# Cosformer attention and a gated MLP on one core: batch 0 in two halves of four heads, chunk 0's first product in units of 128 tokens by four column blocks

## The chip, the cores and the metric

One Trainium2 chip, one core of it. The metric is the device time of one execution in microseconds; less is better. The kernel is written out engine by engine: TensorE (matmuls and their weight loads), VectorE (DVE), ScalarE (ACT), GpSimd (POOL, which here mainly issues loads) and SyncE (SP, which issues stores and transposing DMAs).

## What is computed

Two stages, with 8 batches, 8 heads, 576 positions, head width 64, so 4608 tokens of 512 values; the inner width of the second stage is 2048.

```
def phi(x, c, s):                      # c, s: cos and sin of pi/2 * pos / 576
    r = np.maximum(x, 0.0)
    return np.concatenate([r * c, r * s], axis=-1)
q_p, k_p = phi(q, ...), phi(k, ...)
kv  = einsum('bhsf,bhsd->bhfd', k_p, v);  z = k_p.sum(axis=2)
x   = einsum('bhsf,bhfd->bhsd', q_p, kv) / (einsum('bhsf,bhf->bhs', q_p, z) + 1e-6)
h   = x @ w_in                         # x as [4608, 512], w_in [512, 2048]
out = (h * cos(h)) @ w_out             # w_out [2048, 512]
```

## The kernel before

**Loads.** POOL issues all of them, in the order written, and the values become f16 on the way. K and V of a batch lie as 116 rows of five positions for each head, q as 96 rows of six. Batch 0's loads are split, then come the four column groups of w_in (512 tokens' first product needs all four), two groups of w_out, batch 1, the other two of w_out. Eight semaphores are used in turn, so that a load is issued once the eighth before it has landed.

**Attention of one batch.**
- `scaled` (L143 on DVE, L138 on ScalarE): relu times cos or sin, for one position group `i` of q or k; two instructions each, `t` = 0 and 1.
- `spread_v` (L196, L198): copies V into `vz`, whose 65th column is one, so that the same matmul gives the sum z. For batch 0 there is no such copy: `kv_head` reads a strided view of V and of a block of ones behind it, 128 columns wide (L219).
- `kv_head` (L209, L219): five matmuls for each head into `KV`; after four heads ScalarE copies the result to `kvz` (L224).
- `q_turn` (L167): eight TensorE transposes for one `i` into `QT`, copied to `X` (batch 0 on ScalarE, L186, one `i` at a time; batch 1 two at a time, L181 on ScalarE and L176 on DVE).
- `num_tile` (L235): for 128 tokens, eight matmuls of 65 columns into `NP`; then on DVE `dn` (L242), the reciprocal `rd` (L246) and the product `x` (L255), which `normalise` may issue in two parts.
- `x_turn` (L273): four transposes of `x` into `XP`, copied into `XT` (L281 on ScalarE, L279 on DVE).

From batch 2 on the transposes are DMAs that SP issues.

**The MLP** runs in nine chunks of 512 tokens. M1 (`m1_group`, L288): for each of 16 column blocks of 128 four matmuls of w_in against `XT`; then `co` = cos(M1) on ScalarE (L294) and `g` = M1 · `co` on DVE (L297). M2 (`m2_part`, L307): for each of four token groups `m` sixteen matmuls in four parts, copied by ScalarE to `ost` (L314) and stored by SP. Chunk 0's M1 goes over the 16 blocks twice, 256 tokens at a time, so that it may begin when two token tiles are there.

**Order.** It is written by hand. Chunk c has steps s; `at(c, s, f)` places a piece of attention behind step s, and each engine takes its own instructions in that order. The attention of batches 0 and 1 stands within chunk 0, whose M1 has 32 steps and whose M2 has 16; `z` is the first step of M2. Chunk 1 needs tokens 512 to 1023, that is the last tile of batch 0 and four tiles of batch 1. `warm` issues matmuls on zeros, to keep TensorE running while loads come in.

**PSUM.** `psM` has tags m1 and m2 with two banks each; M1 takes them in turn, M2 of `m` = 0 and 1 takes m2. `psA` has one tag, `att`, with two buffers of two banks, for `QT`, `KV`, `NP` and `XP`.

Of the kernel before, what the change touches and what calls it, by code (L numbers as in the profile page):

```python
# [17 lines left out]
def kernel(  # L18
# [55 lines left out]
    VB = [cpool.tile([PK, H * RUNK + D], F16, name=f"v{n}") for n in "ab"]  # L74
# [23 lines left out]
    def load_q(b, i0=0, i1=R):  # L98
        dst = st[b]["q16"].rearrange("p (h r) -> p h r", h=H)
        nc.gpsimd.dma_start(  # L100
            out=dst[:, :, i0 * D:i1 * D],
            in_=q[b].rearrange("h (p i) d -> p h (i d)", i=R)[:, :, i0 * D:i1 * D],
        )
# [23 lines left out]
    def scaled(b, which, i, h0=0, h1=H):  # L127
        s = st[b]
        rows, n, o = (PR, R, 0) if which == "q" else (PK, RK, R)
        if which + "p" not in s:  # L130
            s[which + "p"] = apool.tile([rows, n, H * F], F16, name=which + "p",
                                        tag=which + "p", bufs=1)
        dst = s[which + "p"][:, i].rearrange("p (h t d) -> p h t d", t=2, d=D)
        src = s[which + "16"][:, 0:H * n * D].rearrange("p (h i d) -> p h i d", i=n, d=D)
        cs = CS[0:rows, :, o + i:o + i + 1]
        for t in range(2):
            if b == 0 and (which == "k" and h0 == 4 and t == 1 or which == "q" and i == 4):
                nc.scalar.activation(  # L138
                    out=dst[:, h0:h1, t, :], in_=src[:, h0:h1, i, :], func=AF.Relu,
                    scale=cs[:, t],  # L140
                )
                continue
            nc.vector.tensor_scalar(  # L143
                out=dst[:, h0:h1, t, :], in0=src[:, h0:h1, i, :],
                scalar1=0.0, scalar2=cs[:, t],
                op0=ALU.max, op1=ALU.mult,
            )

    def q_turn(b, i, tag="m1"):
        s = st[b]  # L150
        if i == 0:
            s["X"] = apool.tile([P, H, S], F16, name="X", tag="X")
        if b >= 2:
            nc.sync.dma_start_transpose(
                out=s["X"][:, :, i * PR:(i + 1) * PR], in_=s["qp"][:, i],
            )
            return
        if b == 1:
            if i % 2 == 0:
                s["QT"] = psA.tile([P, 2, H, P], F16, name="QT", tag="att")  # L160
            QT = s["QT"][:, i % 2]
        elif i >= 4:
            QT = psA.tile([P, 2, H, P], F16, name="QT", tag="att")[:, 0]
        else:
            QT = psM.tile([P, H, P], F16, name="QT", tag=tag)
        for h in range(H):
            nc.tensor.matmul(  # L167
                QT[:, h, 0:PR], lhsT=s["qp"][:, i, h * F:(h + 1) * F], rhs=ID[0:PR, 0:PR],
                is_transpose=True,
            )  # L170
        if b == 1 and i % 2 == 0:
            return
        i0 = i - (b == 1)
        dst = s["X"][:, :, i0 * PR:(i + 1) * PR]
        if b == 1 and i > 1:
            nc.vector.tensor_copy(  # L176
                out=dst.rearrange("p h (a c) -> p a h c", a=2),
                in_=s["QT"][:, :, :, 0:PR],
            )
        elif b == 1:  # L180
            nc.scalar.activation(  # L181
                out=dst.rearrange("p h (a c) -> p a h c", a=2),
                in_=s["QT"][:, :, :, 0:PR], func=AF.Copy,
            )
        else:
            nc.scalar.activation(out=dst, in_=QT[:, :, 0:PR], func=AF.Copy)  # L186

    def spread_v(b, h):
        s = st[b]
        if h == 0:  # L190
            s["vz"] = apool.tile([PK, H, RK, VS], F16, name="vz", tag="vz", bufs=1)
            nc.gpsimd.memset(s["vz"][:, :, :, D:VS], 1.0)
        src = s["v16"][:, 0:H * RUNK].rearrange("p (h i d) -> p h i d", i=RK, d=D)
        dst = s["vz"][:, h:h + 2, :, 0:D]
        if b != 2:
            nc.scalar.activation(out=dst, in_=src[:, h:h + 2], func=AF.Copy)  # L196
        else:
            nc.vector.tensor_copy(out=dst, in_=src[:, h:h + 2])  # L198

    def kv_head(b, h):  # L200
# [5 lines left out]
        n = P if b == 0 else D + 1  # L206
        for i in range(RK):
            if b > 0:
                nc.tensor.matmul(  # L209
                    s["KV"][:, h, 0:n], lhsT=s["kp"][:, i, h * F:(h + 1) * F],  # L210
                    rhs=s["vz"][:, h, i, 0:n], start=(i == 0), stop=(i == RK - 1),
                )
                continue
            base = s["v16"][:, h * RUNK + i * D: h * RUNK + (i + 1) * D]
            vz = bass.AP(
                tensor=base.tensor, offset=base.offset,
                ap=[list(base.ap[0]), [H * RUNK - h * RUNK - i * D, 2], [1, D]],
            )
            nc.tensor.matmul(  # L219
                s["KV"][:, h], lhsT=s["kp"][:, i, h * F:(h + 1) * F], rhs=vz,  # L220
                start=(i == 0), stop=(i == RK - 1),
            )
        if h % 4 == 3:
            nc.scalar.activation(  # L224
                out=s["kvz"][:, h - 3:h + 1], in_=s["KV"][:, h - 3:h + 1, 0:D + 1],
                func=AF.Copy,
            )

# [31 lines left out]
    def x_turn(b, t):  # L260
# [6 lines left out]
        if b == 0 and t < 2:  # L267
            XPf = psM.tile([P, 1024], F16, name="XP", tag="m1")
        else:
            XPf = psA.tile([P, 2048], F16, name="XP", tag="att")  # L270
# [7 lines left out]
        if b == 0 and t == 1:  # L278
# [4 lines left out]
    def m1_group(c, j, n0=0, n1=CH):  # L283
        if ("g", c) not in st:
            st["g", c] = gpool.tile([P, NJT, CH], F16, name="g", tag="g")
        M1 = psM.tile([P, CH], F32, name="M1", tag=("m1", "m2")[j % 2])
        for i in range(NCT):
            nc.tensor.matmul(  # L288
                M1[:, n0:n1], lhsT=w_in_sb[:, i, j * P:(j + 1) * P],
                rhs=XT[:, i, c * CH + n0:c * CH + n1],  # L290
# [4 lines left out]
            out=co[:, n0:n1], in_=M1[:, n0:n1], func=AF.Sin, bias=PIH, scale=1.0,  # L295
        )
        nc.vector.tensor_tensor(  # L297
            out=st["g", c][:, j, n0:n1], in0=M1[:, n0:n1], in1=co[:, n0:n1], op=ALU.mult,
# [31 lines left out]
    HS = NJT  # L330
# [11 lines left out]
    def plan_stage0():  # L342
        at(0, 1, q_turn, 0, 4)
        at(0, 2, scaled, 0, "q", 5)
        at(0, 3, x_turn, 0, 2)
        at(0, 4, loads, 2, "kvq")
        at(0, 6, q_turn, 0, 5)
        for t, n in ((3, 9), (4, HS + 6)):
            at(0, n, num_tile, 0, t, False)
            at(0, n + 1, normalise, 0, t, 0, 1)  # L350
            at(0, n + 2, normalise, 0, t, 1, 2)
            at(0, n + 5, x_turn, 0, t)
        z = 2 * HS
        for i in range(R):
            if i < RK:
                at(0, z + i // 2, scaled, 1, "k", i)
            at(0, z + 3 + i // 2, scaled, 1, "q", i)
        for n in range(4):
            at(0, z + 1 + n, spread_v, 1, 2 * n)
        for h in range(4):  # L360
            at(0, z + 4, kv_head, 1, h)
        for i in range(2):
            at(0, z + 5, q_turn, 1, i)
        for h in range(4, H):
            at(0, z + 5, kv_head, 1, h)
        for i in range(2, R):
            at(0, z + 5 + i // 2, q_turn, 1, i)
        for n, f, t in ((7, num_tile, 0), (8, num_tile, 1), (9, x_turn, 0),
                        (10, num_tile, 2), (10, x_turn, 1), (12, num_tile, 3),
                        (13, x_turn, 2), (14, x_turn, 3), (14, num_tile, 4)):  # L370
            at(0, z + n, f, 1, t)
        at(1, 2, x_turn, 1, 4)
        for i, n in enumerate((9, 10, 11, 12, 13)):
            at(0, z + n, scaled, 2, "k", i)
        for n in range(4):
            at(0, z + 12 + n, spread_v, 2, 2 * n)
# [40 lines left out]
    with tc.manual_schedule():  # L417
# [11 lines left out]
        load_kv(0, "k", 0, 4)  # L429
        load_rest(0, "k")  # L430
        load_kv(0, "k", 4, 8)
        load_q(0, 0, 4)
        for h in range(0, H, 2):
            if h == 2:
                load_rest(0, "v")
            load_kv(0, "v", h, h + 2)
        nc.gpsimd.memset(st[0]["v16"][:, H * RUNK:], 1.0)
        load_w_in(0)
        load_q(0, 4, R)
# [13 lines left out]
        warm(33)  # L453
        for h0 in (0, 4):
            for i in range(RK):
                scaled(0, "k", i, h0, h0 + 4)
        for i in range(4):
            scaled(0, "q", i)
            if i < 2:
                q_turn(0, i)  # L460
        for h in range(8):
            kv_head(0, h)
        q_turn(0, 2, "m2")
        num_tile(0, 0)
        q_turn(0, 3)
        warm(1)
        num_tile(0, 1)
        warm(3)
        x_turn(0, 0)
        warm(2)  # L470
        scaled(0, "q", 4)
        x_turn(0, 1)
        num_tile(0, 2)
        for s in range(2 * HS):
            n = s // HS * (CH // 2)
            m1_group(0, s % HS, n, n + CH // 2)
# [3 lines left out]
        for s, (m, g) in enumerate(order):  # L480
            m2_part(0, m, g)
            run(0, 2 * HS + s)
# [38 lines left out]
```

## Time and profile before

| | us |
|---|---|
| median of 3 runs | 301.39 (300.96 to 301.56) |
| the profiled execution, its own time | 299.56 |
| its span, first to last instruction | 297.8 |
| first matmul of chunk 0's M1 | 19.19 |
| first matmul of chunk 0's M2 | 36.71 |
| first matmul of chunk 1's M1 | 56.52 |

The profile counts time from the first instruction. A line of the timeline is start, length, engine, source line, operation, out<-in, shape, count, and in brackets the idle time before it with what ended it. A group row is a line, engine and operation with its shape and count, then busy time and the mean ns of one, then the idle time before. A DMA row is the number of issues, the KB of one (in f16, as they arrive) and the median time from issue to landing.

### The profile page before, as it was taken

What the parts mean: (1) busy time and instruction counts of PE and PEld (TensorE: products, weight loads), DVE (VectorE), ACT (ScalarE), POOL (GpSimd) and SP (SyncE); (2) the same over time, 40 slices, a digit from 0 to 9 for tenths busy, and PEclk for the clock granted to TensorE, in tenths of its full rate; (3) what the DMA queues carried; (4) which work ended last, traced back from release to release, by engine and by line L of the source; (5) the groups of instructions that cost most, each with busy time, mean ns of one, the idle gap of its engine ahead of it and who ended that gap; (6) DMA issues with size and microseconds to landing.
All of it is one profiled execution on the core that took longest, in us unless ns stands there. A gap on an engine that the chain in (4) does not pass through costs nothing.

```text
span 297.8 us, 5456 instructions
## 1 busy us (share of the span) xinstructions
PE 290.4 (98%) x2031; PEld 150.9 (51%) x2031; DVE 190.3 (64%) x470; ACT 158.7 (53%) x261; POOL 39.8 (13%) x65
## 2 busy tenths in 40 slices
PE   8999999999999999999999999999999999999994
PEld 3577756554544544455445544554455444444441
DVE  1668987988489666966686768677766267007600
ACT  1589952676357624762477158715771177137511
POOL 8733310005004002100210022000000000000000
PEclk9999999999999999999999999999999999999999
DMA  6999999589999996996799959996702610121022
GB/s 89 181 203 206 200 206 200 155 108 134 188 170 147 179 186 117 199 168 130 123 165 181 149 116 169 161 163 136 163 16 70 118 35 0 41 76 28 0 73 70
DMA packets 78019, 38.84 MB, mean 130 GB/s; under 512 B 48296, under 2 KB 73384, under 8 KB 77992
## 3 DMA queue, kind: packets, MB, share of 16 engines
q0 software_dynamic: 28240, 18.36, 44.1%
q1 hardware_dynamic: 49752, 20.13, 38.6%
q8 instruction: 16, 0.26, 0.4%
q14 instruction: 11, 0.09, 0.1%
HBM read 36.76 MB, written 9.44 MB: 155 GB/s over the span
## 4 chain that ended last, share of the span: by engine, by line
PE 89%; DVE 5%; DMA 3%; ACT 1%; POOL 1%; issue 1%; ACTq 0%; POOLq 0%
PE M L307 42%; PE M L288 38%; PE NP L235 3%; DVE g L297 3%; PE KV L209 3%; DMA q<-in_q_dram 3%; PE QT L167 1%; ACT co L294 1%; PE KV L219 1%; PE XP L273 1%; DVE qp L143 1%; POOL ka L108 1%; DVE x L255 0%; PE W L451 0%; POOL ka L115 0%
## 5 line engine op out<-in xcount | busy, mean ns | idle before, releaser
L297 DVE TENSOR_TENSOR g<-M,co 128x512 f16<-128x512 f32 (+1 forms) x160 | 99.9, 635 | 57.5 <-ACT co L294 57.4
L307 PE MATMUL M<-w_out_sb,g 128*128 128x512 f16 x576 | 132.3, 379 | 0.1
L288 PE MATMUL M<-XT,w_in_sb 128*128 128x512 f16 (+1 forms) x640 | 129.5, 358 | 0.6 <-DVE dn L242 0.3
L294 ACT ACTIVATE co<-M,PIH 128x512 f32<-128x512 f32 (+1 forms) x160 | 101.9, 647 | 27.5 <-PE M L288 27.0
L288 PEld LDWEIGHTS <-w_in_sb 128*128 128x128 f16 x640 | 61.3, 98 | 59.7 <-issue 0.9
L307 PEld LDWEIGHTS <-g 128*128 128x128 f16 x576 | 53.8, 98 | 58.7 <-issue 0.3
L314 ACT ACTIVATE ost<-M 128x512 f32<-128x512 f32 x36 | 21.5, 597 | 93.4 <-PE M L307 68.4
L255 DVE TENSOR_TENSOR x<-NP,rd 128x512 f16<-128x512 f32 (+1 forms) x42 | 27.9, 664 | 4.9 <-DMA XT<-x 3.6
L143 DVE TENSOR_SCALAR qp<-q,CS 96x512 f16<-96x512 f16 x94 | 28.5, 350 | 2.1 <-DMA q<-in_q_dram 1.2
L143 DVE TENSOR_SCALAR kp<-ka,CS 116x512 f16<-116x512 f16 (+1 forms) x75 | 21.6, 345 | 5.4 <-DMA ka<-in_k_dram 5.4
L235 PEld LDWEIGHTS <-X 128*128 128x128 f16 x320 | 15.3, 98 | 8.7 <-issue 0.8
L100 POOL DMA_DIRECT2D q<-in_q_dram x9 | 7.0, 779 | 90.8 <-DVE qp L143 88.2
L235 PE MATMUL NP<-kvz,X 128*128 128x65 f16 x320 | 17.0, 194 | 0.2 <-issue 0.2
L242 DVE TENSOR_SCALAR dn<-NP 128x8 f32<-128x8 f32 x40 | 6.5, 162 | 15.4 <-PE NP L235 15.2
L196 ACT ACTIVATE vz<-va 116x640 f16<-116x640 f16 x20 | 13.5, 727 | 0.0
L451 PE MATMUL W<-WU 128*128 128x512 f16 x39 | 12.0, 470 | 1.2 <-DVE PIH L426 1.2
L209 PEld LDWEIGHTS <-kp 116*128 116x128 f16 x280 | 10.7, 98 | 3.1
L209 PE MATMUL KV<-vz,kp 116*128 116x65 f16 x280 | 11.2, 193 | 0.0
L246 DVE RECIPROCAL rd<-dn 128x8 f32<-128x8 f32 x40 | 8.1, 203 | 1.4
L108 POOL DMA_DIRECT2D ka<-in_k_dram x8 | 6.5, 817 | 18.3 <-DVE kp L143 14.9
L451 PEld LDWEIGHTS <-WU 128*128 128x128 f16 x39 | 4.4, 117 | 7.2 <-issue 3.9
L224 ACT ACTIVATE kvz<-KV 128x260 f16<-128x260 f32 x16 | 6.2, 387 | 3.3 <-PE KV L209 2.3
(35 smaller groups left out, 74.5 us busy)
## 6 DMA issues: line engine op xcount, KB each, us to landing
out_dram<-ost SPq DMA_DIRECT2D x24, 192.0 KB, 2.3
q<-in_q_dram POOLq DMA_DIRECT2D x7, 576.0 KB, 7.6
ka<-in_k_dram POOLq DMA_DIRECT2D x6, 560.0 KB, 13.2
va<-in_v_dram POOLq DMA_DIRECT2D x6, 560.0 KB, 11.8
out_dram<-ost SPq DMA_DIRECT2D x24, 128.0 KB, 5.9
w_in_sb<-in_moe_w_in_dram POOLq DMA_DIRECT2D x4, 512.0 KB, 9.9
w_out_sb<-in_moe_w_out_dram POOLq DMA_DIRECT2D x4, 512.0 KB, 16.7
out_dram<-ost SPq DMA_DIRECT2D x24, 64.0 KB, 3.1
```

Source lines behind the costliest of these rows:

```text
L108: nc.gpsimd.dma_start(out=rows_of(st[b][which + "16"])[0:FULL, h0:h1], in_=full[:, h0:h1],)
L143: nc.vector.tensor_scalar(out=dst[:, h0:h1, t, :], in0=src[:, h0:h1, i, :], scalar1=0.0, scalar2=cs[:, t], op0=ALU.max, op1=ALU.mult,)
L196: nc.scalar.activation(out=dst, in_=src[:, h:h + 2], func=AF.Copy)
L209: nc.tensor.matmul(s["KV"][:, h, 0:n], lhsT=s["kp"][:, i, h * F:(h + 1) * F], rhs=s["vz"][:, h, i, 0:n], start=(i == 0), stop=(i == RK - 1),)
L235: nc.tensor.matmul(NP[:, h // 4, o:o + D + 1], lhsT=s["X"][:, h, c0:c0 + P], rhs=s["kvz"][:, h], start=True, stop=True,)
L255: nc.vector.tensor_tensor(out=x4[:, a0:a1], in0=np4[:, a0:a1, :, 0:D], in1=rd[:, a0:a1].broadcast_to((P, a1 - a0, 4, D)), op=ALU.mult,)
L288: nc.tensor.matmul(M1[:, n0:n1], lhsT=w_in_sb[:, i, j * P:(j + 1) * P], rhs=XT[:, i, c * CH + n0:c * CH + n1], start=(i == 0), stop=(i == ...
L294: nc.scalar.activation(out=co[:, n0:n1], in_=M1[:, n0:n1], func=AF.Sin, bias=PIH, scale=1.0,)
L297: nc.vector.tensor_tensor(out=st["g", c][:, j, n0:n1], in0=M1[:, n0:n1], in1=co[:, n0:n1], op=ALU.mult,)
L307: nc.tensor.matmul(M2, lhsT=st["g", c][:, j, m * P:(m + 1) * P], rhs=w_out_sb[:, j], start=(j == 0), stop=(j == NJT - 1),)
L314: nc.scalar.activation(out=ost, in_=M2, func=AF.Copy)
L451: nc.tensor.matmul(W, lhsT=WU[:, 0:P], rhs=WU, start=True, stop=True)
```

## The change

- Batch 0 is loaded in halves of four heads, in the order K, q, V of the first half, then K, q, V of the second (the V of the second in two pieces), then w_in. q comes with all six positions of four heads, where before it came with four positions of all heads and the other two later.
- Batch 0's scalings, transposes (`q_half`, two positions of four heads to a bank), KV products and the first token tile (`first_half`, `first_turn`) are done for each half. Batch 0's V is spread on DVE like that of the other batches, and the ones are set by DVE.
- Chunk 0's M1 runs in 16 units (`m1_unit`): 128 tokens by four column blocks, sixteen matmuls of 128 columns into one bank, one `co` and one `g` of 512 columns. The order of the units is `units`; unit 0 needs token tile 0 alone.
- Token tile 1's and 2's `x_turn` move into M1 (within units 0 and 1), and `num_tile` 2 behind unit 0; `num_tile` 3 stands behind unit 6 and its `x_turn` behind unit 8; tile 4 behind units 9 to 13.
- For batch 1, every odd position of q has its second scaling on ScalarE, and two of the four spread copies go from ScalarE to DVE. Its KV products stand behind steps z+5 and z+6, its transposes behind z+7 to z+9, `num_tile` 0 to 4 behind z+8, 9, 10, 12 and 15 (before: z+4 and z+5; z+5 to z+7; z+7, 8, 10, 12 and 14).
- The opening's matmuls on zeros are 25, then 2, 1, 3, 4 and 2 (before: 33, then 1, 3 and 2).

```diff
-            if b == 0 and (which == "k" and h0 == 4 and t == 1 or which == "q" and i == 4):
+            if t == 1 and (b == 0 and which == "k" and i < (4 if h0 else 3)
+                           or b == 1 and which == "q" and i % 2):
                 nc.scalar.activation(   # scaled, on ScalarE
...
-        if b != 2:
+        if b > 2 or b == 1 and h < 4:
             nc.scalar.activation(out=dst, in_=src[:, h:h + 2], func=AF.Copy)   # spread_v
...
+    def q_half(h0, i, pool, tag):
+        QT = pool.tile([P, 2, 4, P], F16, name="QT", tag=tag)
+        for a in range(2):
+            turn(0, QT[:, a], i + a, h0)
...
+    def m1_unit(u, k_, t):
+        M1 = psM.tile([P, 4, P], F32, name="M1", tag=("m1", "m2")[u % 2])
+        for j in range(4):
+            for i in range(NCT):
+                f0 = (4 * k_ + j) * P
+                nc.tensor.matmul(
+                    M1[:, j], lhsT=w_in_sb[:, i, f0:f0 + P],
+                    rhs=XT[:, i, t * P:(t + 1) * P],
+                    start=(i == 0), stop=(i == NCT - 1),
+                )
+        if u == 0:
+            x_turn(0, 1)
+            num_tile(0, 2)
+        if u == 1:
+            x_turn(0, 2)
+        co = opool.tile([P, 4, P], F32, name="co", tag="co")
+        nc.scalar.activation(out=co, in_=M1, func=AF.Sin, bias=PIH, scale=1.0)
+        nc.vector.tensor_tensor(
+            out=g_for(0)[:, 4 * k_:4 * k_ + 4, t * P:(t + 1) * P], in0=M1, in1=co,
+            op=ALU.mult,
+        )
...
-        load_kv(0, "k", 0, 4)
-        load_rest(0, "k")
-        load_kv(0, "k", 4, 8)
-        load_q(0, 0, 4)
-        for h in range(0, H, 2):
-            if h == 2:
+        ones_for(0, nc.vector)
+        for h0 in (0, 4):
+            load_kv(0, "k", h0, h0 + 4)
+            if h0 == 0:
+                load_rest(0, "k")
+            load_q(0, h0, h0 + 4)
+            if h0 == 0:
+                load_kv(0, "v", 0, 4)
                 load_rest(0, "v")
+        for h in (4, 6):
             load_kv(0, "v", h, h + 2)
-        nc.gpsimd.memset(st[0]["v16"][:, H * RUNK:], 1.0)
         load_w_in(0)
-        load_q(0, 4, R)
...
-        for s in range(2 * HS):
-            n = s // HS * (CH // 2)
-            m1_group(0, s % HS, n, n + CH // 2)
+        units = [(0, 0), (0, 1), (1, 0), (0, 2), (1, 1), (1, 2), (2, 0), (2, 1),
+                 (2, 2), (0, 3), (1, 3), (2, 3), (3, 0), (3, 1), (3, 2), (3, 3)]
+        for s, (g, t) in enumerate(units):
+            m1_unit(s, g, t)
             run(0, s)
```

## The prediction

> **What bounds the kernel now.** I read the page first (its busy line and its chain that ended last), then the busy time by stage, then TensorE's timeline over the opening, and last the groups by shape and the DMA issues for prices.
>
> ```profile
> PE 290.4 (98%) x2031; PEld 150.9 (51%) x2031; DVE 190.3 (64%) x470; ACT 158.7 (53%) x261; POOL 39.8 (13%) x65
> PE 89%; DVE 5%; DMA 3%; ACT 1%; POOL 1%; issue 1%; ACTq 0%; POOLq 0%
> ```
>
> TensorE is the chain for 89% of the span. The change touches only the opening, up to the first instruction of chunk 1; what follows keeps its instructions, so it moves as a block. That block begins at 56.52 us. The stages before it:
>
> ```profile
> core 0: us, PE busy (x) PEld busy (x) DVE busy (x) ACT busy (x) POOL busy (x), PEclk, DMA share, GB/s
> 0.00:19.19 19.19, 17.12 (x144) 9.35 (x145) 8.98 (x34) 8.90 (x16) 13.99 (x24) 1.00 1.08 149
> 19.19:36.71 17.52, 16.68 (x172) 14.19 (x173) 14.69 (x43) 16.33 (x38) 5.16 (x7) 1.00 1.29 204
> 36.71:56.52 19.81, 19.77 (x209) 11.85 (x209) 16.51 (x53) 8.96 (x15) 1.75 (x4) 1.00 1.18 199
> ```
>
> Row one is the opening until the first M1 matmul, row two M1 of chunk 0 (L288), row three its M2 (L307) with batch 1's attention in between. In row two ScalarE is busy 16.33 of 17.52: there the eviction engines, not TensorE, carry the stage. TensorE's timeline gives what the stages consist of:
>
> ```profile
> 11.65 0.52 PE L167 MATMUL QT<-ID,qp 96*128 96x96 f16 x8 [0.23 <-DVE qp L143]
> 12.76 2.40 PE L219 MATMUL KV<-va,kp 116*128 116x128 f16 x40
> 16.67 0.81 PE L451 MATMUL W<-WU 128*128 128x512 f16 x3
> ...
> 28.61 3.22 PE L288 MATMUL M<-XT,w_in_sb 128*128 128x256 f16 x28 [0.25 <-DVE g L297]
> 31.66 0.42 PE L235 MATMUL NP<-kvz,X 128*128 128x65 f16 x8
> ...
> 36.71 4.49 PE L307 MATMUL M<-w_out_sb,g 128*128 128x512 f16 x20
> ```
>
> Pitches follow as (time of the row − time of one matmul) / (count − 1), one lasting 0.19 (65 columns) to 0.38 (512): 0.032 for 65 columns, 0.056 for 128, 0.109 for 256, 0.216 for 512; for 96 columns 0.042, a little under the row, which holds a short wait. A short matmul's result is there about 0.2 us after it starts. Prices on the other engines:
>
> ```profile
> L294 ACT ACTIVATE co<-M,PIH 128x256 f32<-128x256 f32 x32 | 14.0, 485 | 1.0 <-PE M L288 0.8
> L297 DVE TENSOR_TENSOR g<-M,co 128x256 f16<-128x256 f32 x32 | 12.8, 419 | 2.7 <-ACT co L294 2.6
> L288 PEld LDWEIGHTS <-w_in_sb 128*128 128x128 f16 x132 | 12.4, 98 | 2.8 <-issue 0.9
> L255 DVE TENSOR_TENSOR x<-NP,rd 128x512 f16<-128x512 f32 x8 | 5.5, 691 | 0.3
> L281 ACT ACTIVATE XT<-XP 128x512 f16<-128x512 f16 x7 | 4.2, 598 | 1.5 <-PE XP L273 1.3
> L176 DVE COPY X<-QT 128x1536 f16<-128x1536 f16 x2 | 1.9, 958 | 2.8 <-PE QT L167 2.8
> q<-in_q_dram POOLq DMA_DIRECT2D x1, 384.0 KB, 7.5
> q<-in_q_dram POOLq DMA_DIRECT2D x1, 192.0 KB, 8.8
> ```
>
> The 512-column co and g of the later chunks take 0.69 each. Queued instructions start 0.08 to 0.1 before the one ahead of them ends.
>
> **Part 1, loads and opening.** The transfers run back to back at about 200 GB/s from 10 us on, so a load lands by the bytes ahead of it. Before, q's 192 KB are issued at 8.90 and land 8.8 later, at 17.7, with 2,240 KB moved. After, the same 2,240 KB end with w_in's first group, which lands at 17.7; the last V then lands 512 KB earlier, 17.7 − 2.6 = 15.1. Later loads have the same bytes ahead of them and stay. From 15.1, along the new order: DVE's last spread copy to 15.5, twenty KV matmuls (0.64 + 0.2) to 16.1, kvz on ScalarE (0.39) to 16.5, four NP matmuls to 16.85, dn 0.16, rd 0.2, the half x 0.41 to 17.7, two turns to 18.0, the half XT copy. Unit 0 starts with the half turned first, so at about 18.1. The same kind of sum for before, from q's landing, gives 18.8 where the trace has 19.19, so I take 18.4: **−0.8**. The first half (four heads of K and q by about 8.7, V by 10.4) is done well before that and gives only this: M1 needs all eight heads of a token before it can start. Removed warm-up matmuls (33 + 6 to 25 + 12) lie inside waits and cost nothing; if they no longer cover, see the third rival. Spread copies of V replace 128-column KV matmuls: 40 × 0.024 less on TensorE, in the slack of the loads.
>
> **Part 2, M1 in 16 units.** TensorE's work before: 128 × 0.109 + 16 QT × 0.042 + 12 XP × 0.056 + 16 NP × 0.032 = 15.8, so 1.7 of the 17.5 are stalls. After: 256 × 0.056 + 8 × 0.042 + 16 × 0.056 + 24 × 0.032 = 16.35 (two token tiles' turns and one more num_tile moved in). ScalarE falls from 32 × 0.39 to 16 × 0.59, DVE from 32 × 0.34 to 16 × 0.61, so throughput no longer stalls. Latency does, because a unit of 0.9 us now passes through 0.69 + 0.69 before its successor on DVE may go:
> - Unit 1 is token tile 1. Its x is done at about 19.4 by the uncorrected clock (dn, rd, x behind the XT copy of 18.05 to 18.35), its turn at 19.5, the copy on ScalarE at 20.5; unit 0 and num_tile 2 fill part. Stalls 0.15 + 0.3 + 0.6 = 1.05.
> - num_tile 3 stands on DVE behind unit 6's g. From unit 6's last result: co 0.69, g 0.69, dn, rd, x (1.05, with overlaps) = 2.5; TensorE has until the turn NP 0.26 + two units 1.8 = 2.05. Stall with the drain 0.65. The copy to XT then goes behind unit 8's co on ScalarE, 1.05 in all after the turn, against 0.22: stall 0.8 before unit 9, which is token tile 3.
> - Tile 4's turn 0.1.
>
> Sum 16.35 + 2.6 = 19.0: **+1.5**.
>
> **Part 3, M2 and batch 1.** Before: 13.8 (64 M2) + 1.3 (KV) + 2.0 (QT) + 1.3 (NP) + 0.9 (XP) = 19.3, so 0.5 stalls. The same work after, and:
> - M2 of m = 1 takes the bank that unit 15 leaves, 0.2 + 0.69 + 0.69 after that unit's last matmul, with one M2 part of 0.86 in between: 0.8. Before, the halves cost 0.47 + 0.42 there and nothing waited.
> - Batch 1's turns move from the sixth step to the eighth, num_tile from the eighth to the ninth, so DVE's two 0.96 copies fall between the num_tiles. The att banks are two: num_tile 1 waits for x of tile 0, num_tile 2 for x of tile 1, each behind a copy. Stalls 0.15 + 0.3 + 0.6 = 1.05.
> - The shared scalings move three of 0.26 off DVE and put three of 0.61 on ScalarE; two spread copies go the other way. DVE is through with them some 4 us before its first copy of X, ScalarE some 5 us before its own, so they are worth nothing; without that lead the ScalarE part would cost up to 1.3.
>
> Sum 19.3 + 1.9 = 21.2: **+1.4**.
>
> The whole: −0.8 + 1.5 + 1.4 = +2.1. On the profiled execution (span 297.8, own time 299.56) that is a span of 299.9. The median shown, 301.39, is 1.83 above that execution, and I keep the distance: **303.5 us**. Unknown terms: the opening between −1.8 and 0 (landing a microsecond sooner, or no better than now); part 2 between +0.7 and +2.2 (stalls from half to 1.3 times); part 3 between +0.6 and +1.8. They do not go together, so this case's own range is 302.3 to 304.8.
>
> **Rivals.**
> - *The eviction engines were the bound, and relief is all that counts.* For it: ScalarE's 16.33 of 17.52. If the unit order covers all latencies, M1 takes 16.4 and M2 stays 19.8: 18.4 + 16.4 + 19.8 = 54.6 against 56.5, **299.5**. It decides if x of tile 3 is ready within two units after unit 6; the rows make that 2.5 against 2.05. Chance 0.10.
> - *The opening loads land up to 2 us sooner* (q's rows come four heads whole, and the first row moves only 149 GB/s): the start gains up to 2 more, **301.5 to 302.2**, the stalls stay. Chance 0.09.
> - *TensorE loses its full clock in the opening*, whose stream is now more broken (waits of 0.2 to 0.7 between groups from 9 to 18 us). The price is a second warm-up: 33 warm-up matmuls took 10.2 where the later pitch of 0.216 makes 7.3, so +2.9, **306.4**. Against: before, small gaps and transposes between 11.6 and 19 cost nothing, PEclk 1.00. Chance 0.08. The Trainium skill (TensorE: Matmul & The Clock Gate, "Part 4: PE-mode transpose") says that transposes do not count as busy for the clock gate, which speaks for this rival; no row here shows it yet.
> - *The weight loads bound the 128-column matmuls.* Each of the 256 needs a load of its own, and a load lasts 98 ns (the L288 PEld row); at 0.109 a matmul that was covered. If loads could not overlap each other, the pitch would be 0.098 instead of 0.056: 256 × 0.042 = +10.8, **314.3**. Against: the forty KV matmuls, each with its own load, took 2.40 us together, which is 0.056. Chance 0.03. The Trainium skill (TensorE: Matmul & The Clock Gate, "Back-to-back issue gap") gives about 81 ns a matmul for such a sustained stream at N = 128; by it M1 would grow by 6.4 us, an estimate, to 309.9. The trace disagrees, with 56 ns.
>
> **How the numbers follow.** My case has 0.70, the rivals 0.10, 0.09, 0.08 and 0.03. About 0.2%, 0.6 us, is what a measurement here can tell from no change. Faster is the first rival, 0.10; within 0.2% (300.8 to 302.0) most of the second, 0.06; slower the rest, 0.84. The range 301.5 to 305.8 leaves out the first rival, the last and most of the third, some 0.19.
>
> **What would show it.** First M1 matmul near 18.4; turn of tile 3 and unit 9 each with a wait of 0.6 to 0.9; M2 of chunk 0 starting near 37.4 with a break of 0.8 after four matmuls; num_tile 1 and 2 of batch 1 waiting for DVE; chunk 1's M1 near 58.6, and from there the same spacing as before. I am wrong if M1 of chunk 0 takes under 17 us, or if chunk 1 starts before 56.5.

## The result and the profile after

The change makes the kernel slower: 302.49 us (median of 21 runs, 301.99 to 303.88) against 299.95 (median of 21 runs of the kernel before in the same comparison; one of these took 1079.79, the others 298.90 to 303.52), a ratio of 1.0087 [1.0073, 1.0101], or +2.6 us by the ratio. The prediction had +2.1. Its 303.5 lies 1.0 above the measured median, and the starting point is more than all of that: the three runs shown at first, with a median of 301.39, are among the highest of the 21. Set on 299.95, the same sum gives 302.05, which is 0.4 below the measured median.

The profiled execution of after took 302.45 us with a span of 300.6, against 299.56 and 297.8. First the busy line and the chain that ended last, from the page of after:

```profile
PE 289.9 (96%) x2157; PEld 151.8 (51%) x2157; DVE 191.7 (64%) x473; ACT 156.2 (52%) x246; POOL 38.7 (13%) x63
PE 90%; DVE 4%; DMA 2%; ACT 1%; issue 1%; POOL 1%; ACTq 0%; POOLq 0%
```

TensorE is busy for half a microsecond less than before in a span that is 2.8 longer: what was added is waiting. The windows of after by stage (opening, M1 of chunk 0, M2 of chunk 0) answer to the three of before:

```profile
core 0: us, PE busy (x) PEld busy (x) DVE busy (x) ACT busy (x) POOL busy (x), PEclk, DMA share, GB/s
0.00:19.11 19.11, 15.68 (x137) 7.99 (x138) 10.61 (x47) 9.34 (x17) 13.02 (x22) 1.00 1.05 152
19.11:38.17 19.06, 17.28 (x310) 16.46 (x307) 14.47 (x33) 12.25 (x19) 6.50 (x9) 1.00 1.29 203
38.17:59.39 21.22, 20.01 (x212) 11.81 (x210) 15.28 (x47) 10.08 (x17) 0.37 (x3) 1.00 0.99 165
```

Where chunk 1 begins needs one correction. The prediction reckoned with 56.52; the timeline has the first matmul of chunk 1's M1 at 56.35 in before and at 59.39 in after, and that view is used from here on, for all kernels:

```profile
56.35 2.75 PE L288 MATMUL M<-XT,w_in_sb 128*128 128x512 f16 x12
```
```profile
59.39 2.75 PE L337 MATMUL M<-XT,w_in_sb 128*128 128x512 f16 x12
```

So the opening is 0.08 shorter, M1 of chunk 0 is 1.54 longer (19.06 against 17.52) and M2 1.58 longer (21.22 against 19.64): +3.04 where chunk 1 begins. From there to the end of the span there are 241.2 us in after and 241.4 in before.

In M1 ScalarE fell from 16.33 to 12.25 us of busy time, as the change would have it, and the stage still grew. TensorE's timeline of after shows what it waits for:

```profile
19.11 1.23 PE L317 MATMUL M<-XT,w_in_sb 128*128 128x128 f16 x16
20.50 0.40 PE L297 MATMUL XP<-ID,x 128*128 128x128 f16 x4 [0.16 <-DVE x L282]
...
21.58 1.05 PE L317 MATMUL M<-XT,w_in_sb 128*128 128x128 f16 x16 [0.43 <-ACT XT L305]
...
22.70 2.84 PE L317 MATMUL M<-XT,w_in_sb 128*128 128x128 f16 x48
...
27.77 1.95 PE L317 MATMUL M<-XT,w_in_sb 128*128 128x128 f16 x32
30.21 0.40 PE L297 MATMUL XP<-ID,x 128*128 128x128 f16 x4 [0.50 <-DVE x L282]
31.30 1.05 PE L317 MATMUL M<-XT,w_in_sb 128*128 128x128 f16 x16 [0.69 <-ACT XT L305]
...
38.17 1.03 PE L356 MATMUL M<-w_out_sb,g 128*128 128x512 f16 x4
39.84 4.48 PE L356 MATMUL M<-w_out_sb,g 128*128 128x512 f16 x20 [0.64 <-DVE g L329]
...
53.62 0.43 PE L262 MATMUL NP<-kvz,X 128*128 128x65 f16 x8 [0.46 <-DVE x L282]
```

Each bracket is idle time, and each one names the step that comes late: tile 1's `x` and its copy to `XT` (20.50, 21.58), tile 3's (30.21, 31.30), `g` of unit 15 (39.84), batch 1's `x` behind a copy on DVE (53.62). A bracket counts from the modelled end of the matmul before; by the prediction's pitches the gaps are larger. After 32 matmuls of 0.056 from 27.77, for example, TensorE is free at 29.56 and stands until 30.21, 0.65.

### The profile page after: what moved, and what is told of

The parts are those of the page before. It is cut to its first block, busy times and chain, and to the rows that moved or that the text cites. A ratio compares the mean times of both kernels' runs of the same rounds, so it can differ in the third digit from the quotient of the medians.

```text
span 300.6 us, 5679 instructions
## 1 busy us (share of the span) xinstructions
PE 289.9 (96%) x2157; PEld 151.8 (51%) x2157; DVE 191.7 (64%) x473; ACT 156.2 (52%) x246; POOL 38.7 (13%) x63
## 4 chain that ended last, share of the span: by engine, by line
PE 90%; DVE 4%; DMA 2%; ACT 1%; issue 1%; POOL 1%; ACTq 0%; POOLq 0%
PE M L356 41%; PE M L337 37%; PE M L317 4%; PE KV L212 3%; PE NP L262 3%; DMA va<-in_v_dram 2%; PE QT L172 1%; DVE x L282 1%; PE XP L297 1%; DVE X L166 1%; DVE g L329 0%; ACT co L328 0%; DVE qp L144 0%; ACT XT L305 0%; DVE x L237 0%
## 5 line engine op out<-in xcount | busy, mean ns | idle before, releaser
L346 DVE TENSOR_TENSOR g<-M,co 128x512 f16<-128x512 f32 x128 | 87.1, 689 | 53.8 <-ACT co L343 53.7
L337 PE MATMUL M<-XT,w_in_sb 128*128 128x512 f16 x512 | 113.9, 379 | 0.0
L343 ACT ACTIVATE co<-M,PIH 128x512 f32<-128x512 f32 x128 | 88.0, 688 | 26.7 <-PE M L337 25.9
L337 PEld LDWEIGHTS <-w_in_sb 128*128 128x128 f16 x512 | 49.1, 98 | 57.2
L144 DVE TENSOR_SCALAR qp<-q,CS 96x512 f16<-96x512 f16 (+1 forms) x105 | 29.9, 338 | 0.9 <-DMA X<-qp 0.9
L282 DVE TENSOR_TENSOR x<-NP,rd 128x512 f16<-128x512 f32 (+1 forms) x40 | 27.1, 678 | 4.7 <-DMA XT<-x 3.4
L317 PE MATMUL M<-XT,w_in_sb 128*128 128x128 f16 x256 | 15.8, 219 | 1.1 <-ACT XT L305 1.1
L317 PEld LDWEIGHTS <-w_in_sb 128*128 128x128 f16 x256 | 14.7, 98 | 1.5 <-issue 1.3
L212 PEld LDWEIGHTS <-kp 116*128 116x128 f16 x320 | 12.3, 98 | 4.4 <-ACT X L185 1.1
L212 PE MATMUL KV<-vz,kp 116*128 116x65 f16 x320 | 12.8, 193 | 1.0 <-DVE vz L203 1.0
L328 ACT ACTIVATE co<-M,PIH 128x512 f32<-128x512 f32 x16 | 11.0, 687 | 5.0 <-PE M L317 4.8
L329 DVE TENSOR_TENSOR g<-M,co 128x512 f16<-128x512 f32 x16 | 10.9, 687 | 3.8 <-ACT co L328 3.5
## 6 DMA issues: line engine op xcount, KB each, us to landing
w_out_sb<-in_moe_w_out_dram POOLq DMA_DIRECT2D x4, 512.0 KB, 16.4
```

Source lines behind the costliest of these rows:

```text
L144: nc.vector.tensor_scalar(out=dst[:, h0:h1, t, :], in0=src[:, h0:h1, i, :], scalar1=0.0, scalar2=cs[:, t], op0=ALU.max, op1=ALU.mult,)
L212: nc.tensor.matmul(s["KV"][:, h, 0:D + 1], lhsT=s["kp"][:, i, h * F:(h + 1) * F], rhs=s["vz"][:, h, i, 0:D + 1], start=(i == 0), stop=(i = ...
L282: nc.vector.tensor_tensor(out=x4[:, a0:a1], in0=np4[:, a0:a1, :, 0:D], in1=rd[:, a0:a1].broadcast_to((P, a1 - a0, 4, D)), op=ALU.mult,)
L317: nc.tensor.matmul(M1[:, j], lhsT=w_in_sb[:, i, f0:f0 + P], rhs=XT[:, i, t * P:(t + 1) * P], start=(i == 0), stop=(i == NCT - 1),)
L337: nc.tensor.matmul(M1, lhsT=w_in_sb[:, i, j * P:(j + 1) * P], rhs=XT[:, i, c * CH:(c + 1) * CH], start=(i == 0), stop=(i == NCT - 1),)
L343: nc.scalar.activation(out=co, in_=M1, func=AF.Sin, bias=PIH, scale=1.0,)
```

## The experiments

Ratios are against the kernel before, measured alongside on the same chip; edits are against after unless said otherwise.

**1. The order of the units.** Tile 3 is needed two units later, and its turn stands one step later.

```diff
-        at(0, 8, x_turn, 0, 3)
+        at(0, 9, x_turn, 0, 3)
...
-                 (2, 2), (0, 3), (1, 3), (2, 3), (3, 0), (3, 1), (3, 2), (3, 3)]
+                 (2, 2), (3, 0), (3, 1), (0, 3), (1, 3), (2, 3), (3, 2), (3, 3)]
```

> Changed kernel with two column blocks of tiles 0 and 1, (3,0) and (3,1), moved ahead of (0,3), and tile 3's turn one unit later. Theory 'exposed latency': the waits before tile 3's turn (0.5) and before unit 9 (0.7) vanish, M1 of chunk 0 falls from 19.1 to about 17.6, the whole by 1.3 to 1.5 against the changed kernel, so about 0.4% over the kernel before. Rival 'the units themselves are dearer on TensorE' (128-column matmuls, more weight loads): the matmuls are the same, M1 stays at 19.1 and the time at 302.5, 0.9% over.

Measured 301.12 us, 1.0043 [1.0014, 1.0073]. The windows of M1 and M2 of chunk 0:

```profile
17.98:35.53 17.55, 16.96 (x309) 16.45 (x306) 14.47 (x33) 12.14 (x19) 5.71 (x8) 1.00 1.29 204
35.53:56.75 21.22, 20.01 (x211) 11.82 (x209) 15.56 (x47) 10.30 (x17) 1.75 (x4) 1.00 1.14 189
```

M1 takes 17.55 instead of 19.06, so the 1.5 at tile 3 are the latency of one token tile, with the same work on every engine. M2 is not touched: 21.22 again. The start at 17.98 is discussed below.

**2. The order of M2's first parts.** Two parts each of m = 0 and m = 1 would run from the start; here m = 0 has two first.

```diff
-        order = [(m, g) for p in (0, 2) for g in range(2) for m in (p, p + 1)]
+        order = [(0, 0), (0, 1), (1, 0), (1, 1), (2, 0), (3, 0), (2, 1), (3, 1)]
```

> Changed kernel with M2's first parts in the order (0,0), (0,1), (1,0), (1,1), so that the second part needs no bank of the last M1 unit. Theory 'exposed latency': the break of 0.8 after four M2 matmuls goes, -0.8, so 0.6% over the kernel before. Rival 'the bank is not what it waits for, but g': the wait only moves to a later part, no change, 0.9% over.

Measured 301.81 us, 1.0061 [1.0036, 1.0086]. The window of M2 of chunk 0:

```profile
37.39:57.80 20.41, 19.84 (x211) 11.81 (x209) 15.27 (x47) 10.19 (x17) 1.45 (x4) 1.00 1.06 177
```

20.41 instead of 21.22: the wait for unit 15's bank was worth 0.81.

**3. Batch 1's steps as in before**, the shared scalings and copies left as the change has them.

```diff
-        for h in range(H):
-            at(0, z + 5 + h // 4, kv_head, 1, h)
-        for i in range(R):
-            at(0, z + 7 + i // 2, q_turn, 1, i)
+        for h in range(4):
+            at(0, z + 4, kv_head, 1, h)
+        for i in range(2):
+            at(0, z + 5, q_turn, 1, i)
+        for h in range(4, H):
+            at(0, z + 5, kv_head, 1, h)
+        for i in range(2, R):
+            at(0, z + 5 + i // 2, q_turn, 1, i)
-        for n, f, t in ((8, num_tile, 0), (9, num_tile, 1), (10, x_turn, 0),
-                        (10, num_tile, 2), (11, x_turn, 1), (12, num_tile, 3),
-                        (12, x_turn, 2), (14, x_turn, 3), (15, num_tile, 4)):
+        for n, f, t in ((7, num_tile, 0), (8, num_tile, 1), (9, x_turn, 0),
+                        (10, num_tile, 2), (10, x_turn, 1), (12, num_tile, 3),
+                        (13, x_turn, 2), (14, x_turn, 3), (14, num_tile, 4)):
```

> Changed kernel with batch 1's KV products, turns and num_tiles back at the steps of the kernel before; the shared scalings stay. Theory 'exposed latency': num_tile 1 and 2 no longer wait behind DVE's copies, M2 stage from 21.2 to about 20.4, -0.8, 0.6% over the kernel before. Rival 'the shared scalings cost it': they stay, so nothing changes, 0.9% over.

Measured 301.74 us, 1.0064 [1.0043, 1.0085]. The window of M2 of chunk 0:

```profile
37.33:57.76 20.43, 19.76 (x211) 11.76 (x209) 14.98 (x46) 9.95 (x16) 1.72 (x4) 1.00 1.08 181
```

0.79 of the 1.58 are batch 1's later steps. With the 0.81 of experiment 2, all of M2's growth is accounted for.

**4. Later loads held back.** In the opening, DVE's scalings last longer in after than their length elsewhere. This edit makes POOL issue w_out and batch 1 only after DVE's scalings of the second half.

```diff
-        load_w_out(0)
...
+        nc.vector.memset(HOLD, 0.0)
+        nc.gpsimd.memset(HOLD, 0.0)
+        load_w_out(0)
+        load_w_out(1)
+        loads(1, "kvq")
...
```

> Changed kernel in which POOL issues w_out and batch 1's loads only after DVE's last scaling of batch 0's second half (a 128x1 memset on DVE and one on POOL hold it), while the w_in loads still fill the queue. Theory 'DVE is slowed while POOL issues': the copies and scalings between 14.6 and 16.3 us take 0.7 less, M1 starts at about 18.4 instead of 19.1, -0.7 in all, 0.6 to 0.7% over the kernel before. Rival 'the second half simply lands too late': M1 still starts at 19.1, 0.9% over, or later if the held loads come late.

Measured 302.54 us, 1.0079 [1.0048, 1.0109]. DVE's timeline, after first:

```profile
14.65 1.29 DVE L144 TENSOR_SCALAR qp<-q,CS 96x256 f16<-96x256 f16 x4
15.46 0.88 DVE L203 COPY vz<-va 116x640 f16<-116x640 f16 x2
```
```profile
14.69 0.86 DVE L145 TENSOR_SCALAR qp<-q,CS 96x256 f16<-96x256 f16 x4
15.48 0.55 DVE L204 COPY vz<-va 116x640 f16<-116x640 f16 x2
```

The second pair is the kernel that holds the loads: four scalings in 0.86 instead of 1.29, two copies in 0.55 instead of 0.88. The last V lands at 15.36 in after and at 15.33 here, so the 0.38 by which M1 begins earlier (18.73) does not come from the loads' landing; the 0.76 that DVE saves is the difference seen on the way. But the time does not fall by the expected amount: in chunk 2, near 112 us, TensorE waits 0.56, where after has no wait. That wait is taken up below.

**5. The four edits together** (1, 2, 3 and 4).

> Changed kernel with the four edits at once: unit order, M2 order, batch 1's steps, held loads. Theory 'exposed latency': they add, 1.5 + 0.8 + 0.8, with 0.4 of the held loads 3.5 in all; chunk 1 starts near 55.5, and the time is 0.3% under the kernel before, less what the wait for a transposing DMA near 110 us gives back (0.1 to 0.9 in the runs so far). Rival 'the stalls share one cause': less than 2 together, still slower than before.

Measured 299.70 us, 0.9987 [0.9970, 1.0004]. Against after that is 1.0% less; the four single ratios add up to 0.44 + 0.26 + 0.23 + 0.08 = 1.0%. Chunk 1 begins at 55.57, 3.82 earlier than in after:

```profile
55.57 2.75 PE L338 MATMUL M<-XT,w_in_sb 128*128 128x512 f16 x12
```

The stalls at tile 3, at unit 15's bank and in batch 1, 3.1 us together, explain the slowdown: without them the kernel is no slower than before. The stall at tile 1 is still there, with gaps of 0.48 and 0.59. The kernel isn't clearly faster than before either, though chunk 1 begins 0.78 earlier.

**6. The units alone.** The kernel before, its loads, opening and batch 1's steps kept, with chunk 0's M1 in the 16 units in an order that lets tile 3 come late, and M2's parts as in experiment 2. The edit is against before:

```diff
...
+        at(0, 0, q_turn, 0, 4)
+        at(0, 1, scaled, 0, "q", 5)
+        at(0, 1, x_turn, 0, 2)
+        at(0, 2, loads, 2, "kvq")
+        at(0, 3, q_turn, 0, 5)
+        for t, n in ((3, 5), (4, 10)):
...
+        units = [(0, 0), (0, 1), (1, 0), (1, 1), (0, 2), (1, 2), (2, 0), (2, 1),
+                 (2, 2), (3, 0), (3, 1), (0, 3), (1, 3), (2, 3), (3, 2), (3, 3)]
+        for s, (g, t) in enumerate(units):
+            m1_unit(s, g, t)
             run(0, s)
-        order = [(m, g) for p in (0, 2) for g in range(2) for m in (p, p + 1)]
+        order = [(0, 0), (0, 1), (1, 0), (1, 1), (2, 0), (3, 0), (2, 1), (3, 1)]
```

> Kernel before, its opening with all heads at once, with only M1 of chunk 0 in the sixteen units, in an order whose copies are ready (tile 2's units from the fifth, tile 3's from the twelfth), and M2's first parts in the order of the second experiment. Theory 'relief of ScalarE and DVE is real, exposed latency took it away': M1 stage from 17.5 to about 16.7, M2 stage as before, so 0.8 to 1.4 faster than the kernel before (0.3 to 0.5%). Rival 'units are no gain in any order': the same as the kernel before or slower.

Measured 298.70 us, 0.9959 [0.9933, 0.9985]: faster than both kernels, and the best of this study. Its windows of M1 and M2:

```profile
18.45:35.16 16.71, 16.69 (x306) 16.17 (x303) 13.29 (x29) 13.69 (x22) 5.40 (x8) 1.00 1.29 204
35.16:54.91 19.75, 19.72 (x212) 11.80 (x209) 16.54 (x53) 9.39 (x15) 1.78 (x4) 1.00 1.25 209
```

TensorE is busy for 16.69 of 16.71. Here the first rival's mechanism comes true: with every latency covered, tile 1's too, and ScalarE at 13.69 instead of 16.33, M1 falls 0.81 below before. Chunk 1 begins at 54.91, 1.44 earlier than in before, and 0.74 of that lies ahead of M1. From DVE's first scaling of q to M1 there are 7.69 us, in before 8.20: unit 0 needs token tile 0 alone, which saves 0.5 with the old loads. The rest is q landing earlier in this execution.

**7. The same with w_in's later groups and all loads behind them held** until DVE's eight scalings of q are through.

```diff
-        for g in range(1, 4):
-            load_w_in(g)
...
+        nc.vector.memset(HOLD, 0.0)
+        nc.gpsimd.memset(HOLD, 0.0)
+        for g in range(1, 4):
+            load_w_in(g)
...
```

> The sixth experiment's kernel, in which POOL issues w_in's groups 1 to 3 and all later loads only after DVE's first eight scalings of q. In the kernel before four of these took 0.56 to 0.59 instead of 0.34 while POOL was issuing, so the first M1 matmul comes 0.6 to 0.9 earlier than in the sixth, and 0.2% more is gained, if the loads still land in time. Rival 'loads then come late': unit 2 waits for w_in group 1 and the gain is gone.

Measured 299.32 us, 0.9984 [0.9962, 1.0007]. The eight scalings take 2.19 us instead of 2.88, yet M1 begins at 18.64 and not earlier. In this execution q landed later: DVE's scalings start at 11.17 instead of 10.76. From there to M1 there are 7.47 us instead of 7.69, so the hold saves 0.2, where 0.6 to 0.9 was expected. That is less than the landing differs by, and no gain in the time is seen.

**8. The kernel before, once more**, one execution.

> The kernel before, unchanged, for a second trace of its opening: four traces whose opening is that of the changed kernel have their first M1 matmul at 18.0 to 19.1. If the opening's gain of 0.8 is real, this one is near 19.2 again; if before varies as much, it is anywhere from 18.3 to 19.5.

Measured 300.4 us. M1 begins at 19.94, later than either forecast and 0.75 later than in the first trace of the same kernel, as the first part of q lands at 11.71 instead of 10.96; M1 takes 17.75 and M2 19.63. The opening of one trace is thus known to some tenths only.

**9. The sharing for batch 1 undone**: all scalings of q on DVE, all four copies of V on ScalarE.

```diff
-            if t == 1 and (b == 0 and which == "k" and i < (4 if h0 else 3)
-                           or b == 1 and which == "q" and i % 2):
+            if t == 1 and (b == 0 and which == "k" and i < (4 if h0 else 3)):
...
-        if b > 2 or b == 1 and h < 4:
+        if b != 2 and b != 0:
```

> Changed kernel with batch 1's scalings and spread copies divided as in the kernel before (all q scalings on DVE, all copies of V on ScalarE). Theory 'off the path': DVE is through with them some 4 us before its first copy of X, so nothing moves, 0.8 to 0.9% over the kernel before. Rival 'the shared scalings make ScalarE late in the M2 stage': 0.3% or more better than the changed kernel.

Measured 303.31 us, 1.0132 [1.0106, 1.0158], four runs. M1 takes 19.06 and M2 21.22, to the hundredth what they take in after, so the shared scalings are off the path, as forecast. The time is longer all the same: chunk 1 begins at 58.80, and in chunk 2 TensorE waits 1.29 at 112.58. Why this wait is larger here than in the other kernels was not found.

**10. The halves alone.** After's loads and opening, but M1 in 32 steps of 256 tokens and batch 1's steps as in before.

```diff
-        for s, (g, t) in enumerate(units):
-            m1_unit(s, g, t)
+        x_turn(0, 1)
+        num_tile(0, 2)
+        for s in range(2 * NJT):
+            n = s // NJT * (CH // 2)
+            m1_half(0, s % NJT, n, n + CH // 2)
...
```

> Changed kernel's loads and opening in two halves of four heads and its shared scalings, but M1 of chunk 0 in halves of 256 tokens and batch 1's steps as in the kernel before. Theory 'the earlier first matmul comes from needing one token tile, not from the halves': M1 needs tiles 0 and 1 again, starts about 1.3 later than in the kernel before, near 20.5, and the time is 0.3 to 0.5% over it. Rival 'the halves bring the 0.8': M1 starts near 18.5 and the time is 0.2% under.

Measured 302.17 us, 1.0085 [1.0055, 1.0115], six runs from 301.04 to 303.64; the profiled one, 303.59, is of the upper end. M1 begins at 20.94, close to the forecast: it needs a second token tile, and in this opening that tile comes 2.5 us behind the first. So the earlier start of after comes from needing one tile, and not from the halves. The time misses its forecast of 0.3 to 0.5%. In the profiled execution TensorE also loses its full clock. Two windows, before and after the change of clock (PEclk is the third number from the end):

```profile
18.00:21.40 3.40, 1.66 (x27) 1.39 (x28) 2.13 (x8) 0.60 (x1) 0.60 (x2) 1.00 1.24 206
21.40:24.81 3.41, 3.41 (x21) 2.56 (x19) 2.17 (x8) 1.89 (x4) 1.10 (x2) 0.50 1.24 206
```

In the 3.4 us ahead TensorE was busy for 1.66, with waits of 0.50, 1.22 and 0.43; then it ran at 0.50 for 3.41 us. That is the third rival's mechanism, which did not occur in after.

**11. Buffers in turn.** Experiment 6 with K and V buffers alternating from batch to batch, so that a batch's loads can be issued a chunk earlier, out of the way of the transposes near 110 us. Edit against experiment 6:

```diff
-        odd = int(b == 1)
+        odd = b % 2
...
-        at(1, 9, loads, 3)
+        at(0, z + 12, loads, 3)
...
-        if 1 < c and c + 2 < B:
-            at(c, 4, loads, c + 2)
+        if c + 3 < B:
+            at(c, 9, loads, c + 3)
```

> The sixth experiment's kernel with the two sets of K, V and q buffers used in turn by all batches (before: the second only by batch 1) and each batch's loads issued about a chunk earlier. Theory 'TensorE's wait near 110 us comes from transposing DMAs that share the queues with batch 4's loads': the wait for X in chunk 2 is gone in the trace, 0.1 to 0.5 faster than the sixth experiment, 0.4 to 0.6% under the kernel before. Rival 'the transposes are slow by themselves, or SP issues them late': the wait stays between 0 and 1.4, the time near that of the sixth.

Measured 303.11 us, 1.0106 [1.0077, 1.0135], where a gain was expected. The wait came back in chunk 1, and larger; TensorE's timeline, and the windows around it:

```profile
79.63 0.42 PE L235 MATMUL NP<-kvz,X 128*128 128x65 f16 x8 [2.63 <-issue]
```
```profile
76.80:80.20 3.40, 0.77 (x11) 0.48 (x11) 0.34 (x2) 0.00 (x0) 0.00 (x0) 1.00 1.33 187
80.20:83.61 3.41, 3.41 (x17) 1.47 (x15) 1.75 (x7) 1.85 (x3) 0.00 (x0) 0.51 1.23 218
```

The last transpose X<-qp was issued from 69.12 to 70.89, behind batch 4's loads (issued from 66.40 to 69.98), and landed at 79.54, just before the matmul that reads it could go. The wait then also cost the clock, 0.51 for 3.41 us.

**12. The same buffers and loads with the edits of experiment 5.**

> The fifth experiment's kernel (all four edits) with the buffers in turn and the earlier loads. Theory: its wait of 1.2 near 110 us goes, so 1.2 less, about 0.5% under the kernel before. Rival: the wait stays and with it 0.1% under.

Measured 299.24 us, 0.9982 [0.9960, 1.0004]. Here the wait near 110 is gone and no other takes its place, but the ratio is only 0.05% below that of experiment 5, well within its interval, and the 0.5% of the forecast is missed. So even without that wait the opening in halves is no better than the units alone.

## Why the prediction came out as it did

**The opening, −0.8: right in size as a rule, 0.7 short in the profiled pair, and its two possible causes not parted.** After's own trace begins M1 at 19.11, the forecast was 18.4. Experiments 1, 2, 3 and 9 leave after's opening as it is, and begin at 17.98, 18.33, 18.27 and 18.52; with 19.11 the mean is 18.44. The two traces of before begin at 19.19 and 19.94, both 8.23 after the first part of q has landed. So the pair of traces that was compared first is an extreme one.

The prediction added up the new opening from the last V's landing, and did not part its two changes: the loads in halves, and a first unit that needs one token tile. The runs do. Experiments 6, 7 and 11 have before's loads and opening and a first unit that needs one tile, and begin M1 at 18.45, 18.64 and 18.28, as early as after's opening. Experiment 10 has the halves and needs two tiles, and begins at 20.94. So the gain comes from needing one tile, and no gain of the halves is seen. What the new opening does is leave tile 1 late: the stall there, which the prediction counted under M1 with 1.05, is absent in experiment 6.

Two things spread the starts of after's opening. The last V lands at 15.36 in after and between 14.50 and 14.85 in the other four (forecast 15.1). And the sum took DVE's scalings and copies at their plain length, while in after they ran beside POOL issuing loads, 1.29 instead of 0.86 for four scalings; in the pair of after and experiment 4, M1 begins 0.38 earlier without that. The chain from the last V to M1 was forecast at 3.0 (to 18.1) or 3.3 (to the 18.4 taken). With the loads held (experiments 4, 5 and 12) it is 3.3 to 3.5; without, 3.1 to 3.9 (3.75 in after). How much of the spread is DVE's stays open.

The Trainium skill (SBUF — State Buffer, "Who interferes with whom") says that VectorE in its two-port mode and GpSimd share one pair of ports, that whoever comes first keeps it for its whole instruction, and that GpSimd needs it for writing descriptors. The trace agrees: scalings and copies, from SBUF to SBUF, stretch, while `x` of 256 columns, which reads PSUM, takes 0.42 with the loads and without. Not every operation stretches: in experiment 1 the same four scalings took 0.86 while POOL was issuing, and one of POOL's issues took 1.18 instead of 0.83.

**M1, +1.5: right, and for its reasons.** Reckoned by the prediction's pitches, the gaps in after's timeline are 0.49 and 0.59 at tile 1 (forecast 1.05 together), 0.65 at tile 3's turn (0.65), 0.87 before unit 9 (0.8) and none at tile 4 (0.1): 2.6 against 2.6. Experiment 1 took 1.51 away by order alone. The fourth rival, the weight loads, is refuted by the same timeline: 48 matmuls of 128 columns in 2.84 us are 0.056 each, as in before's KV row.

**M2, +1.4: right, 1.58 on the timeline's starting point.** After four M2 matmuls TensorE stands from 39.03 to 39.84, 0.81 (forecast 0.8). Batch 1's gaps are 0.17, 0.29 and 0.63 (0.15, 0.3 and 0.6). Experiments 2 and 3 took away 0.81 and 0.79, and the shared scalings are worth nothing in the stage (experiment 9). The only term off is the stall of before, put at 0.5; with chunk 1 at 56.35 it is 0.3.

**"What follows moves as a block": true for this pair, not in general.** Between the first M1 matmuls of chunks 2 and 3 there are 30.33 us in after, 30.51 in before, 31.24 in experiment 1 and 31.57 in experiment 5. What gives is one `num_tile` of batch 3, in experiment 1:

```profile
110.12 0.42 PE L262 MATMUL NP<-kvz,X 128*128 128x65 f16 x8 [0.88 <-issue]
```

It reads `X`, whose last transposing DMA is issued behind batch 4's loads and lands late. In experiment 7 the trace names this DMA as what ended the wait:

```profile
108.90 0.42 PE L236 MATMUL NP<-kvz,X 128*128 128x65 f16 x8 [1.13 <-DMA X<-qp]
```

The DMA issues of experiment 1 between 85 and 115 us, of before in the same stretch, and of before over its whole span:

```profile
X<-qp SPq DMA_TRANSPOSE x6, 10.9
```
```profile
X<-qp SPq DMA_TRANSPOSE x7, 10.8
```
```profile
X<-qp SPq DMA_TRANSPOSE x36, 4.0
```

The last number is the median from issue to landing. In this stretch it is 10.8 to 10.9 us, against 4.0 over the whole kernel, and in before and after it is as slow as in experiment 1. The wait is 0.15 in before, nothing in after, and 0.88, 0.56 and 1.21 in experiments 1, 4 and 5. In experiment 5 it took back 1.2 of the gain. How early the opening ends does not decide it: experiments 6 and 12 begin chunk 1 at 54.91 and 56.01 and do not wait, experiments 9 and 10 begin it at 58.80 and 59.17 and wait 1.29 and 0.81. What does decide it was not found.

**The rivals.** The first was right about the units and wrong about this change: its M1 of 16.4 needed an order in which tile 3 is not asked for within two units, as the prediction's condition said, and also a tile 1 that is ready. Experiment 1 met the first alone and has 17.55; experiment 6 met both and has 16.71. The second, loads landing sooner, came to 0.3 to 0.6 us in four traces and not in after's. The third did not occur in after, whose clock is 1.00 in every stage; the loss of the clock did occur in experiment 10, in the opening, and in experiment 11, in chunk 1. The Trainium skill (TensorE: Matmul & The Clock Gate, "What's actually happening") gives a free-running window of 3.41 us, and half clock after an idle one. The 3.41 us at 0.50 and 0.51 agree with its length; the window ahead of them was not idle but busy for 1.66 and 0.77.

## What to carry to other kernels

Finer pieces relieve an engine that is busy for 93% of a stage. That is worth something only if the pieces keep dependent steps apart: TensorE must have as much work between the instruction that starts a chain and the one that needs its end as the chain takes. Count that work for each piece. Here the same units cost 1.5 us in one order, nothing in a second, and gained 0.8 where tile 1 was ready too. When two changes go in together, ask of each what it brings alone: the earlier start came from the single tile and not from the halves. And do not take it that what follows moves as a block: a wait of 0 to 1.3 us a chunk later came and went between kernels with the same instructions there.

## What was not expected of the hardware

- VectorE's f16 scalings and copies from SBUF to SBUF can stretch while GpSimd issues a load: four of 256 columns took 1.29 us instead of 0.86, two copies of 640 columns 0.88 instead of 0.55.
- Transposing DMAs issued among GpSimd's loads landed 9.0 to 11.8 us after their issue (medians between 85 and 115 us of the traces), against 4.0 over the whole kernel before.
- TensorE went to half clock for 3.41 us after 3.4 us in which it was busy for 1.66 and its longest wait was 1.22.
- The opening of the same program differs by 0.75 us from one execution to the next.
